# Expert 0 of a mixture of experts, started tile by tile inside the rounds of a linear attention

## The chip, the cores and the metric

One core of one Trainium2 chip. The time is device time of one launch in microseconds, the median of several runs; less is better. Profiles are of one further execution.

## The reference

A linear attention with decay feeds a mixture of experts. Sizes: 4 batches, 8 heads, 768 steps, head width 48; then 3072 tokens of width 384, 8 experts with hidden width 1024. All arrays are float32.

```python
for t in range(S):                       # attention, per batch and head
    cur = einsum('bhd,bhe->bhde', u * kt, vt)
    y[:, :, t] = einsum('bhd,bhde->bhe', rt, state + cur)
    state = w * state + einsum('bhd,bhe->bhde', kt, vt)
x = y.transpose(0, 2, 1, 3).reshape(3072, 384)
P = exp(x @ w_gate - max)                # gate
for _ in range(8):                       # Sinkhorn: rows, then columns
    P /= P.sum(1, keepdims=True) + 1e-9
    P /= P.sum(0, keepdims=True) + 1e-9
    P *= N / E
for e in range(E):                       # every expert on every token
    out += P[:, e:e+1] * (relu(x @ w1[e]) @ w2[e])
```

The gate needs all tokens, so it is known only after the whole attention. An expert's two products need only their tokens.

## The kernel before

**Tiles and rounds.** The 3072 tokens are 24 tiles of 128. Six tiles make a batch; the state S is carried from tile to tile within one. A loop of 27 rounds runs over the tiles with a lag, so that round i works on several tiles:

- `load_chunk(i+4)`: three DMAs on SyncE's queue for r, k, v of tile i+4. There are three buffers each for r and k and five for v, so the load of v waits until `stage_d(i-1)`, in the same round, is through with v of tile i-1.
- `prep(i+2)`: r and k times the decay tables `rtab` and `ktab` (r on GpSimd, k on VectorE: `rp`, `kp`).
- `bonus_dot(i+1)`, `bonus(i)`: the term with u, mostly GpSimd. It also adds `xadd`, the part of `hbx` that has been cleared to zero (the branch below may put something there).
- `stage_b(i+1)`: transposition of `rp` and `kp` on TensorE (`prT`, `pkT`), copied out by ScalarE.
- `scale_x(i-2)`, `stage_e(i-2)`: x of tile i-2 is split into a high and a low float16 part (`xsc`), and a DMA on SyncE's queue transposes it into `hbx`.
- `stage_c(i)`: products `pA` of transposed k and r, masked copies into `at` (VectorE), and the state's update (`pu`, S).
- `stage_d(i-1)`: `py`, the tile's output, on TensorE; then x, its largest magnitude and its scale on VectorE.
- `stage_f(i-3)`: the gate's logits `px`.

Every engine keeps the order in which the program issues its work, SyncE's queue too. The transposed blocks, `pA`, `pu` and `py` take turns in four PSUM banks.

**Expert 0 in the rounds.** TensorE is filled up with units of expert 0 (`work(n)`). Weights and activations are split into high and low float16 parts, so that each product takes three matmuls. `g1_unit(po, fc)` makes 128 of the 1024 hidden columns for position po, which is three tiles: 9 matmuls of 384 columns into `ph`, then ReLU on ScalarE (`hh`) and its low part on VectorE (`hl`). `g2_half(po, t, j)` multiplies half j of the hidden columns of one tile by w2: 12 matmuls into `po`, a copy and a DMA to `e0d`. Units of a position are listed when its three tiles are transposed. Units are worked on from round 5 on, two a round until round 8 and three from round 9 on; in earlier rounds `work` runs `spin(3)`, three matmuls on zeros that keep TensorE busy. What is left after the rounds runs in a loop that also does the Sinkhorn steps, and ten units and a rest inside the stages of the other experts.

**Steps beside the rounds.** `prepare()` takes the next step of a list; `STEPS` says how many steps a round takes before and after `stage_d`. First w1 of expert 0 is prepared, then w2 (largest magnitude in three pieces, reduction, exchange over partitions, scale, then high parts on ScalarE and low parts on VectorE), then combinations of tokens for the other experts (GpSimd additions). The latter begin in round 9.

**Start.** `hbx` is cleared by three engines. The tables come from a scan of w's powers on VectorE (`step`, `unit`, `pw`) and a reciprocal of all powers (`iv`), are transposed on TensorE (`pt_tab`) and copied out by ScalarE. If a decay lies outside [0.7, 1.1], a branch on `flag` (line 430) runs the attention of those channels step by step in `scan_channels`. With these inputs it isn't taken.

```python
for i in range(NTT + 3):
    ...
    work(1, i > 4)                 # after stage_e(i - 2)
    ...                            # bonus(i), stage_c(i)
    if i <= NTT:
        work(2 if i > 8 else 1, i > 4)
    ...                            # steps, stage_d(i - 1), steps, stage_f(i - 3)
    done = i - 2                   # the tile transposed in this round
```

Of the kernel before, what the change touches and what calls it, by code (L numbers as in the profile page):

```python
# [8 lines left out]
F32 = mybir.dt.float32  # L9
# [23 lines left out]
def rwkv_sinkhorn_moe(  # L33
# [117 lines left out]
    def split_weights(e, r1, r2, home):  # L151
# [11 lines left out]
        def rest_():  # L163
            pass

        for raw, wh, wl, j in ((r1, w1h, w1l, 0), (r2, w2h, w2l, 1)):
# [19 lines left out]
            def high(i, fl=fl, j=j, n=n):  # L186
                sl = slice(i * n, (i + 1) * n)
                S_.activation(fl[1][:, sl], fl[0][:, sl], AF.Copy, scale=sw[:, j : j + 1])

            def low(i, fl=fl, j=j, n=n):  # L190
                sl = slice(i * n, (i + 1) * n)
                V.scalar_tensor_tensor(
                    fl[2][:, sl], fl[0][:, sl], sw[:, j : j + 1], fl[1][:, sl],
                    op0=ALU.mult, op1=ALU.subtract,
                )

            steps = [lambda i=i, f=amax: f(i) for i in range(KC)] + [reduce_max, rest_, across, rest_, scale]
            for i in range(KC + 1):
                fs = [lambda i=i, f=high: f(i)] if i < KC else []
                fs += [lambda i=i, f=low: f(i - 1)] if i else []  # L200
                if i >= KC - 1:
                    fs.append(lambda i=i, j=j: split_done.add((("w1", "w2")[j], i - KC + 1)))
                steps.append(lambda fs=fs: [f() for f in fs])
            pieces += steps
# [9 lines left out]
    def g1_unit(po_, fc, W):  # L214
# [3 lines left out]
        hh, hl = h0(fc // FHC)  # L218
        ph = ps1.tile([P, TB], F32, tag="ph", name=f"ph_{po_}_{fc}")[:, :TB0]
# [3 lines left out]
        for c in range(KC):  # L223
# [6 lines left out]
            if c == KC - 1:  # L230
                fl = fc % FHC
                S_.activation(hh[:, fl, :], ph, AF.Relu)
                V.scalar_tensor_tensor(
                    hl[:, fl, :], ph, 0.0, hh[:, fl, :], op0=ALU.max, op1=ALU.subtract
                )
            yield

# [22 lines left out]
    def whole(gen):  # L260
        for _ in gen:
            pass
# [14 lines left out]
    wrow = part(hb3, F32, 2112, (H, D))[:1]  # L277
    wr = w.rearrange("(p two) d -> two d p", two=2)
    S_.dma_start(wrow, w.rearrange("(o h) d -> o h d", o=1))
# [14 lines left out]
    loads = {}  # L294

    def load_part(tt, nm, src):
        b, c = divmod(tt, NCHB)
        if tt == 3 and nm != "v":
            t_ = part(hb3, F32, 2880 + "rk".index(nm) * H * D, (H, D))
        else:  # L300
            t_ = ld.tile([P, H, D], F32, tag=nm + "n", name=f"{nm}n_{tt}", bufs=5 if nm == "v" else 3)
# [7 lines left out]
    raws = (part(ws0, F32, 0, (KC, F)), part(ws0, F32, KC * F, (FC, DM)))  # L309
    for tt in range(2):  # L310
        load_part(tt, "r", r)
        load_part(tt, "k", k)

    ub = ac.tile([P, H, D], F32, name="ub")
    wg = ac.tile([P, KC, E], F32, name="wg")

    load_part(0, "v", v)
# [3 lines left out]
    )  # L321
    load_part(2, "r", r)
    load_part(2, "k", k)
    load_part(1, "v", v)
    load_part(3, "r", r)
    load_part(3, "k", k)
    Q.dma_start(wg, w_gate.rearrange("(c p) e -> p c e", p=P))
    for c in range(KC):
        Q.dma_start(raws[0][:, c], w1[0, c * P : (c + 1) * P, :])


    N1 = HP + 1
    tmp = hb3
    step, unit, pw, iv = (
        tmp[:, i * NPAIR * N1 : (i + 1) * NPAIR * N1].rearrange("p (a n) -> p a n", n=N1)
        for i in range(4)
    )
    G.memset(hbx[:, :HB], 0.0)
# [3 lines left out]
    V.memset(hbx[:, HB : 2 * HB], 0.0)  # L342
# [8 lines left out]
    fill(hbx[:, 2 * HB :])  # L351
    spin(19)
# [8 lines left out]
    )  # L361
    maski = mask.bitcast(I32)
# [8 lines left out]
    for t_ in ss_:  # L371
        for j in range(2):
            G.memset(t_[j * HP : (j + 1) * HP, :, 1 - j, :], 0.0)
# [4 lines left out]

    wlim = part(hb3, F32, 2496, (H, D))[:1]
    flag = ac.tile([1, 1], F32, name="flag")  # L380
    V.tensor_scalar(wlim, wrow, W_MAX, W_MIN, op0=ALU.min, op1=ALU.max)
    V.tensor_tensor(wlim, wlim, wrow, op=ALU.not_equal)
    V.tensor_reduce(flag, wlim, axis=AX.XY, op=ALU.max)


    def scan_channels(scratch):
# [7 lines left out]
        Q.dma_start(wn, w.rearrange("(o h) d -> o (h d)", o=1).broadcast_to([D, H * D]))  # L394
# [12 lines left out]
        with tc.For_i(0, S, 1) as t:  # L407
            for dst, src in ((kb, k), (rb, r)):
                Q.dma_start(
# [3 lines left out]
            Q.dma_start(vt, v.rearrange("b h s d -> s d (b h)")[bass.ds(t, 1)].rearrange("o d a -> (o d) a"))  # L413
            V.tensor_tensor(rb, rb, stt, op=ALU.mult)
            V.tensor_reduce(yv, rb, axis=AX.X, op=ALU.add)
            for b in range(B):
                Q.dma_start(
# [8 lines left out]
        for t in range(NTT):  # L426
            Q.dma_start(xadd(t), yt[:, t, :])

    bad = nc.values_load(flag.bitcast(I32), min_val=0, max_val=0x3F800000)
    with tc.If(bad > 0):  # L430
# [3 lines left out]
    load_part(2, "v", v)  # L434
    load_part(3, "v", v)


    wsafe = ac.tile([P, NPAIR], F32, name="wsafe")
    good = ac.tile([P, NPAIR], F32, name="good")
    V.tensor_scalar(wsafe, wt, W_MAX, W_MIN, op0=ALU.min, op1=ALU.max)  # L440
    V.tensor_copy(step[:, :, 1:], wsafe.unsqueeze(2).broadcast_to([P, NPAIR, HP]))
    V.tensor_tensor_scan(
        pw.rearrange("p a n -> p (a n)"), step.rearrange("p a n -> p (a n)"),
        unit.rearrange("p a n -> p (a n)"), 0.0, op0=ALU.mult, op1=ALU.add,
    )

    V.tensor_tensor(good, wt, wsafe, op=ALU.is_equal)
    V.reciprocal(iv, pw)
    tab, tabr = (part(hb3, F32, 1040 + i * NPAIR * C, (NPAIR, C)) for i in range(2))
# [806 lines left out]
```

## Time and profile before

| what | value |
|---|---|
| median of 3 runs | 1536.81 us (1536.73 to 1538.33) |
| the profiled execution | 1537.3 us, its span 1535.4 us |
| TensorE (PE) busy | 1519.8 us, 99% of the span |
| VectorE (DVE) | 1033.7 us, 67% |
| ScalarE (ACT) | 663.5 us, 43% |
| GpSimd (POOL) | 598.1 us, 39% |
| DMA | 143.12 MB, mean 93 GB/s |

All operations of the kernel are recorded on one line, L29 (the helper that keeps program order), so groups are told apart by the names of their tiles. An arrow `a<-b` reads: a is written from b. A bracket at a row's end gives the engine's idle time before it and what ended it. Matmuls are pipelined; the pitch from one start to the next tells more than the length of one. SP is SyncE, and a q behind an engine's name is its instruction queue.

### The profile page before, as it was taken

What the parts mean: (1) busy time and instruction counts of PE and PEld (TensorE: products, weight loads), DVE (VectorE), ACT (ScalarE), POOL (GpSimd) and SP (SyncE); (2) the same over time, 40 slices, a digit from 0 to 9 for tenths busy, and PEclk for the clock granted to TensorE, in tenths of its full rate; (3) what the DMA queues carried; (4) which work ended last, traced back from release to release, by engine and by line L of the source; (5) the groups of instructions that cost most, each with busy time, mean ns of one, the idle gap of its engine ahead of it and who ended that gap; (6) DMA issues with size and microseconds to landing.
All of it is one profiled execution on the core that took longest, in us unless ns stands there. A gap on an engine that the chain in (4) does not pass through costs nothing.

```text
span 1535.4 us, 26169 instructions
## 1 busy us (share of the span) xinstructions
PE 1519.8 (99%) x10313; PEld 858.1 (56%) x10313; DVE 1033.7 (67%) x1714; ACT 663.5 (43%) x1168; POOL 598.1 (39%) x708
## 2 busy tenths in 40 slices
PE   8999999999999999999999999999999999999999
PEld 5677766655555555555555555555555555555555
DVE  8988877676666666667666666656666566666554
ACT  4333424434444444535454444535344444445320
POOL 8789985120213424242424324242423224242200
PEclk9999999999999999999999999999999999999999
DMA  8556623121225665675666666655445554555434
GB/s 192 104 114 113 131 49 112 51 73 55 98 58 109 88 118 86 110 107 83 116 92 125 92 117 88 126 64 98 58 62 92 61 98 56 98 60 98 55 95 129
DMA packets 186847, 143.12 MB, mean 93 GB/s; under 512 B 109537, under 2 KB 180962, under 8 KB 186722
## 3 DMA queue, kind: packets, MB, share of 16 engines
q0 software_dynamic: 44928, 61.36, 32.6%
q1 hardware_dynamic: 141584, 80.07, 19.8%
q8 instruction: 81, 1.33, 0.4%
q14 instruction: 44, 0.36, 0.1%
q10 hardware_dynamic: 210, 0.00, 0.0%
HBM read 55.39 MB, written 80.23 MB: 88 GB/s over the span
## 4 chain that ended last, share of the span: by engine, by line
PE 94%; DVE 5%; issue 0%; ACT 0%; DMA 0%; DVEq 0%; ACTq 0%
PE po L29 48%; PE bZ L29 12%; PE bY L29 12%; PE ph L29 5%; PE bA L29 5%; PE bB L29 5%; PE bC L29 2%; PE py L29 2%; PE pA L29 1%; DVE hb L29 1%; PE prT L29 1%; PE pu L29 1%; DVE at L29 0%; DVE ws L29 0%; PE pkT L29 0%
## 5 line engine op out<-in xcount | busy, mean ns | idle before, releaser
L29 PE MATMUL po<-ws,hbx 128*128 128x384 f16 x3360 | 736.8, 326 | 0.0
L29 POOL DMA_DIRECT2D accd<-stg x288 | 249.7, 869 | 694.4 <-ACT stg L29 673.8
L29 PEld LDWEIGHTS <-hbx 128*128 128x128 f16 x3504 | 334.1, 98 | 292.6
L29 PEld LDWEIGHTS <-ws 128*128 128x128 f16 x3096 | 301.8, 98 | 246.7 <-issue 3.4
L29 ACT ACTIVATE hbx<-tb 128x512 f16<-128x512 f32 x224 | 141.0, 630 | 451.6 <-DVE tb L29 451.6
L29 PE MATMUL po<-ws,hb 128*128 128x384 f16 x1248 | 323.0, 326 | 0.3 <-DVE ws L29 0.3
L29 DVE TENSOR_TENSOR tb<-bY,tb 128x512 f32<-128x512 f32 x168 | 116.1, 691 | 195.4 <-PE bY L29 195.2
L29 ACT ACTIVATE stg<-po,pe 128x384 f32<-128x384 f32 x312 | 179.1, 574 | 121.2 <-PE po L29 94.3
L29 PE MATMUL bZ<-xv,ws 128*128 128x512 f16 x840 | 227.0, 379 | 0.7 <-DVE tb L29 0.7
L29 PE MATMUL bY<-xv,ws 128*128 128x512 f16 x840 | 227.0, 379 | 0.0
L29 DVE TENSOR_TENSOR tb<-bZ,tb 128x512 f32<-128x512 f32 x168 | 115.4, 687 | 136.3 <-PE bZ L29 136.3
L29 PEld LDWEIGHTS <-hb 128*128 128x128 f16 x1248 | 121.4, 98 | 93.8 <-issue 0.8
L29 POOL TENSOR_TENSOR ucb<-rawb 128x256 f32<-128x256 f32 x84 | 75.7, 952 | 118.7 <-DMA rawb<-in_moe_w_dram 118.7
L29 DVE TENSOR_TENSOR tb<-bB,tb 128x512 f32<-128x512 f32 x112 | 77.4, 691 | 48.9 <-PE bB L29 47.0
L29 PE MATMUL ph<-hbx,ws 128*128 128x384 f16 x576 | 105.8, 329 | 1.2 <-DMA hbx<-xsc 0.7
L29 DVE SCALAR_TENSOR_TENSOR hb<-tb,hbx 128x512 f16<-128x512 f32 x112 | 77.2, 689 | 24.7 <-ACT hbx L29 19.5
L29 PE MATMUL bB<-xv,ws 128*128 128x512 f16 x336 | 90.8, 379 | 0.0
L29 PE MATMUL bA<-xv,ws 128*128 128x512 f16 x336 | 90.8, 379 | 0.0
L29 DVE SCALAR_TENSOR_TENSOR hbx<-tb,hbx 128x512 f16<-128x512 f32 x112 | 78.7, 703 | 14.7 <-ACT hbx L29 10.4
L29 ACT COPY tb<-bZ 128x512 f32<-128x512 f32 x56 | 32.8, 585 | 65.5 <-PE bZ L29 65.5
L29 ACT ACTIVATE hb<-ph 128x384 f16<-128x384 f32 x64 | 31.1, 488 | 57.6 <-PE ph L29 57.0
L29 DVE SCALAR_TENSOR_TENSOR hb<-ph,hb 128x384 f16<-128x384 f32 x64 | 35.4, 553 | 26.3 <-ACT hb L29 25.8
(166 smaller groups left out, 1539.6 us busy)
## 6 DMA issues: line engine op xcount, KB each, us to landing
accd<-stg POOLq DMA_DIRECT2D x288, 192.0 KB, 3.7
rawb<-in_moe_w_dram SPq DMA_DIRECT2D x28, 768.0 KB, 6.7
e0d<-stg SPq DMA_DIRECT2D x48, 192.0 KB, 2.1
hb<-e0d SPq DMA_DIRECT2D x48, 192.0 KB, 3.9
vn<-in_v_dram SPq DMA_DIRECT2D x24, 192.0 KB, 3.6
accd<-stg SPq DMA_DIRECT2D x24, 192.0 KB, 1.8
accd<-hb POOLq DMA_DIRECT2D x24, 192.0 KB, 4.7
rawb<-accd SPq DMA_DIRECT2D x24, 192.0 KB, 2.5
```

The lines of the kernel that those rows point to most:

```text
L29: return lambda *a, **k: self.tc.keep_in_program_order(f(*a, **k))
```

## The change

**Start.** The tables are built ahead of the branch in the program. One scan now runs over w and 1/w together, so the reciprocal is taken of w alone. The flag comes from the same columns through a small matmul on ones (`pnb`) instead of from a row of w of its own. VectorE clears five tiles of `hbx`, GpSimd eleven in pieces, ScalarE the last eight; VectorE also clears the state's off-diagonal blocks. The branch's DMAs are issued by GpSimd instead of SyncE.

**Loads.** All loads of tiles 0 to 4, r and k of tile 5, and both weights of expert 0 are issued ahead of the branch, w1's three pieces among tiles 0 and 1. r and k of tiles 3, 4 and 5 get places of their own (`hb3`, `xv0`). v of tile 5 is loaded in round 1, and from round 2 on round i loads tile i+4 as before.

**w1 and w2.** High and low parts are made in two pieces instead of three, each a half of the hidden columns. A first step stands behind `prep(0)`, a second behind `prep(1)`, and the new `STEPS` has w1 ready at the end of round 2, the first half of w2 at the end of round 5 and the second in round 6. In round 0 the order of `prep`, `bonus` and `stage_b` differs.

**Expert 0.** Position 0 is done tile by tile: `g1_tile(t, j)` makes half j of the hidden columns of tile t with 36 matmuls of 128 columns into one bank. Two of them are listed in the round in which tile t is transposed, and `work` uses them from round 3 on: tile t in round t+3, once ahead of `stage_c` and once after. The six `g2_half` of position 0 follow in rounds 6 to 8. Rounds 9 to 11 now have two units instead of three; from round 12 on there are three. ReLU and the low part of a unit are issued later, by `leave()`: ahead of the next unit, or behind the steps that precede `stage_d`.

```diff
@@ split_weights
+            def half(x_, i, j=j):
+                return x_[:, i * FHC : (i + 1) * FHC] if j else x_[:, :, i * FH : (i + 1) * FH]
...
+            pieces += [lambda i=i, f=amax: f(i) for i in range(KC)] + [reduce_max, across, scale]
+            pieces += [lambda f=high: f(0), lambda h=high, l=low: (h(1), l(0)), lambda f=low: f(1)]
@@ new
+    def g1_tile(t, j, W):
...
+        ph = ps1.tile([P, TB], F32, tag="ph", name=f"pht_{t}_{j}")
+        ph = ph.rearrange("p (f q) -> p f q", q=P)
+        for fl in range(FHC):
+            fs = slice((j * FHC + fl) * P, (j * FHC + fl + 1) * P)
+            for c in range(KC):
+                xh_, xl_ = xall(t, 0)[:, c, :], xall(t, 1)[:, c, :]
+                T.matmul(ph[:, fl], w1h[:, c, fs], xh_, start=(c == 0), stop=False)
+                T.matmul(ph[:, fl], w1h[:, c, fs], xl_, start=False, stop=False)
+                T.matmul(ph[:, fl], w1l[:, c, fs], xh_, start=False, stop=(c == KC - 1))
+        exits.append((hh, hl, ph))
+    def leave():
+        while exits:
+            hh, hl, ph = exits.pop(0)
+            S_.activation(hh, ph, AF.Relu)
+            V.scalar_tensor_tensor(hl, ph, 0.0, hh, op0=ALU.max, op1=ALU.subtract)
@@ whole(gen)
+        leave()
@@ loads
     for tt in range(2):
         load_part(tt, "r", r)
         load_part(tt, "k", k)
+    load_w1(0)
     ...                              # u
     load_part(0, "v", v)
+    load_w1(1)
+    load_w1(2)
+    load_part(1, "v", v)
     load_part(2, "r", r)
     load_part(2, "k", k)
     ...                              # w_gate
+    load_part(2, "v", v)
+    for tt in (3, 4):
+        load_chunk(tt)
+    Q.dma_start(raws[1], w2[0].rearrange("(c p) d -> p c d", p=P))
+    load_part(5, "r", r)
+    load_part(5, "k", k)
@@ start
-    G.memset(hbx[:, :HB], 0.0)
-    V.memset(hbx[:, HB : 2 * HB], 0.0)
+    V.memset(hbx[:, : Z[1]], 0.0)
+    clear_tiles(5, 11)
...
-    V.reciprocal(iv, pw)
+    V.reciprocal(wsi[:, 1], wsafe)
@@ scan_channels
-                Q.dma_start(
+                G.dma_start(
@@ rounds
     STEPS = {
-        0: (2, 2), 1: (0, 2), 2: (3, 1), 3: (1, 1),
-        4: (1, 1), 5: (1, 1), 6: (2, 2), 7: (1, 1), 8: (1, 1),
+        0: (3, 0), 1: (0, 2), 2: (1, 1), 3: (2, 1), 4: (1, 0), 5: (1, 3), 6: (1, 0), 7: (0, 0), 8: (0, 0),
     }
+    FIRST = TH
...
-        work(1, i > 4)
+        work(1, i >= FIRST)
...
-            work(2 if i > 8 else 1, i > 4)
+            work(2 if i > 11 else 1, i >= FIRST)
...
+        leave()
         if 1 <= i <= NTT:
             stage_d(i - 1)
...
+        if 0 <= done < TH:
+            units += [g1_tile(done, j, W) for j in range(2)]
+        if done == TH - 1:
+            units += [g2_half(0, t, j, W) for j in range(2) for t in range(TH)]
```

186 lines of the change are left out of this document (95 added, 91 removed).

## The prediction

> **What bounds the kernel now.** I read the page's busy times and slices first, then busy time by stretch, then TensorE's order of work, and last SyncE's queue. The page:
>
> ```profile
> PE 1519.8 (99%) x10313; PEld 858.1 (56%) x10313; DVE 1033.7 (67%) x1714; ACT 663.5 (43%) x1168; POOL 598.1 (39%) x708
> ```
>
> TensorE is the bound nearly everywhere; where it isn't must lie in the 1% left, which the next view finds at the front. I cut the front at each round's first transposition (prT): round 3 begins at 32.35, round 4 at 43.09, round 5 at 50.82, round 6 at 60.30, round 9 at 83.43, round 12 at 113.39. Columns of the next view: stretch, length, then busy us of each engine with its instructions, granted TensorE clock, DMA share, GB/s.
>
> ```profile
> 14.88:32.35 17.47, 16.96 (x281) 12.63 (x280) 16.92 (x32) 5.01 (x9) 16.92 (x18) 1.00 0.84 235
> 32.35:43.09 10.74, 8.12 (x117) 5.72 (x117) 9.96 (x24) 5.01 (x7) 8.86 (x10) 0.84 0.89 167
> 50.82:60.30 9.48, 8.73 (x113) 5.55 (x113) 9.25 (x19) 2.77 (x5) 7.14 (x10) 0.82 0.38 73
> 60.30:83.43 23.13, 22.52 (x377) 16.91 (x374) 22.10 (x51) 10.58 (x18) 15.59 (x17) 1.00 0.54 105
> 83.43:113.39 29.96, 29.62 (x419) 21.11 (x417) 25.86 (x50) 9.88 (x19) 25.26 (x26) 1.00 0.55 107
> 113.39:300.00 186.61, 186.11 (x2129) 126.19 (x2126) 150.46 (x302) 74.77 (x136) 134.50 (x147) 1.00 0.43 94
> 300.00:1500.00 1200.00, 1199.32 (x6559) 641.98 (x6558) 767.42 (x1188) 542.87 (x958) 374.15 (x455) 1.00 0.54 88
> ```
>
> From 83.43 on TensorE idles 0.34 + 0.50 + 0.68 us in 1417. So the change is worth this and little else: when round 9 begins, and how much expert-0 work ("units") is done by then. Before that VectorE sets the pace (22.10 of 23.13 us in rounds 6 to 8), TensorE having only two units a round. One full round and two halves of w2 products give the prices (start, length; the pitch is the distance to the next start):
>
> ```profile
> 75.87 0.64 PE L29 MATMUL prT<-ident,rp 128*128 128x128 f32 x4
> 76.34 0.60 PE L29 MATMUL pkT<-ident,kp 128*128 128x128 f32 x4
> 76.78 1.63 PE L29 MATMUL ph<-hbx,ws 128*128 128x384 f16 x9
> 78.33 1.10 PE L29 MATMUL pA<-rT,kT 64*64 64x128 f32 x32
> 79.37 0.67 PE L29 MATMUL pu<-vn,kp 128*64 128x48 f32 x16
> 79.97 1.64 PE L29 MATMUL ph<-hbx,ws 128*128 128x384 f16 x9
> 81.54 0.88 PE L29 MATMUL py<-S,rT 128*64 128x96 f32 x16
> 82.25 1.09 PE L29 MATMUL py<-vn,at 128*64 128x48 f32 x32
> 83.27 0.30 PE L29 MATMUL px<-wgp,hbx 128*128 128x16 f16 x6
> 88.59 4.06 PE L29 MATMUL po<-ws,hb 128*128 128x384 f16 x24
> ```
>
> Round 8 is 7.56: two w1 units of 1.55 and 1.57, and 4.44 of attention. Two w2 half units take 4.06 with the tail of the pipeline, 2.0 each. Without pu (a batch's last tile) attention is 3.84, without py from S (its first) 3.73.
>
> **The change, part by part.** The unit counts first. Before, 8 w1 units of position 0 run in rounds 5 to 8. After, six tile units run in rounds 3 to 5 and all six w2 halves of position 0 in rounds 6 to 8; rounds 9 to 11 then have two units instead of three. From round 9 on 104 units remain before and 98 after: six w2 halves fewer, 6 x 2.0 = **-12.0 us**. That is the whole gain on offer; all else is when round 9 begins.
>
> *Start and tables.* These rows carry the table chain and its consumers:
>
> ```profile
> 2.27 2.62 DVE L29 MEMSET hbx<- 128x3072 f32 x1 [0.59 <-issue]
> 6.98 0.17 DVE L29 TENSOR_SCALAR wsafe<-wt 128x4 f32<-128x4 f32 x1 [0.74 <-DVE flag L29]
> 7.53 0.70 DVE L29 TENSOR_TENSOR_SCAN hb<-hb 128x260 f32<-128x260 f32 x1
> 8.96 1.76 DVE L29 RECIPROCAL hb<-hb 128x260 f32<-128x260 f32 x1
> 14.03 3.16 DVE L29 TENSOR_TENSOR kp<-kn,ktab 128x384 f32<-128x384 f32 x3 [1.98 <-ACT ktab L29]
> 31.47 1.36 DVE L29 COPY_PREDICATED at<-mask,pA 128x512 f32<-128x512 int32 x2
> ```
>
> The clearing shrinks to 1920 of 3072 columns (-0.98), the 260-column reciprocal to 4 columns (-1.6), the scan doubles (+0.7): kp of tile 0 at 12.1. If the 2.09 us between the clearing's end (4.89) and wsafe leave the chain too, 10.0. I take 11. From there to the end of tile 2's masked copies was 18.8 us; the same work stands there after (the three maxima of w1 included), plus a wait for r2 and k2, which now queue behind all of w1. I take 19.5: round 3 at 30.5 (29 to 32; before 32.35). POOL's clearings (16 tiles less five on VectorE and eight on ScalarE) stay ahead of its first use of a table.
>
> *The loads.* SyncE's queue, and the DMA rate in 40 slices of 1.5 us:
>
> ```profile
> 12.79 1.77 SPq L29 DMA_DIRECT2D ws<-in_moe_w_dram  x3
> 21.02 1.28 SPq L29 DMA_DIRECT2D vn<-in_v_dram  x2
> 37.62 1.49 SPq L29 DMA_TRANSPOSE hbx<-xsc  x1
> ...
> L430 SPq EVENT_SEMAPHORE  x8: 17/17/17, 18.7 to 20.6; - x8
> L430 DVEq COMPARE_BRANCH  x1: 67/67/67, 14.0 to 14.0; - x1
> ...
> GB/s 0 16 218 213 183 176 147 198 198 158 339 404 270 3 39 152 236 189 172 373 383 292 132 170 218 129 170 169 89 119 154 20 223 131 150 5 0 67 197 9
> ```
>
> At the branch SyncE sits from 14.56 to 21.02 and the DMAs stand still for some 2.5 us (the slices 3 and 39). With the branch's DMAs moved to POOL and all loads ahead of it I count that as gone. But tile 0's transposition, the first input of expert 0, still has seven tiles' r, k, v and both weights ahead of it on that queue: 37.62, less 2.5, plus 3.1 to landing = **38.2** (36 to 41). In the kernel before, nothing waited for it then.
>
> *Round 3.* TensorE has its transpositions done at 31.4 and then stands at the first tile unit until 38.2, with pA of tile 3 queued behind it. Then 36 matmuls of 128 columns. No row has that form. Below lies px, 0.16/6 = 0.027 each for 16 columns; above, 0.172 for 384. A third of the latter is 0.057; I take 0.060, 2.2 a unit (1.0 to 6.2). So round 4 begins at 38.2 + 2.2 + 1.04 + 0.60 + 2.2 + 1.73 + 0.16 = 46.1: **+3.0** (-0.2 to +6). On the warm price alone the Trainium skill speaks ("TensorE: Matmul & The Clock Gate", "Wait — 56ns, not 53.3ns?"): about 55.6 ns from start to start for 128 columns, by which a unit would be an estimated 2.0 us; no run here shows it yet.
>
> *Rounds 4 and 5.* The lag is what costs. The load of v(i+4) waits on SyncE's queue for py(i-1) of the same round (five buffers), and tile i-2 is transposed behind it:
>
> ```profile
> 48.86 0.31 PE L29 MATMUL px<-wgp,hbx 128*128 128x16 f16 x6
> 50.82 0.63 PE L29 MATMUL prT<-ident,rp 128*128 128x128 f32 x4 [1.65 <-DVE at L29]
> 52.76 0.50 PE L29 MATMUL ph<-hbx,ws 128*128 128x384 f16 x1 [0.75 <-DMA hbx<-xsc]
> 48.97 0.37 SPq L29 DMA_DIRECT2D vn<-in_v_dram  x1
> 49.60 1.22 SPq L29 DMA_TRANSPOSE hbx<-xsc  x1
> ```
>
> py is over when px starts at 48.86, v goes at 48.97, the transposition at 49.60 lands at 52.76: 3.6 to 3.9 us. TensorE reaches the first unit of the next round 0.16 + 0.91 = 1.1 after py. Before, that hit once; after, each of rounds 4 and 5 opens with the tile just transposed and waits 2.5. Round 4: 4.44 + 4.4 + 2.5 = 11.3; round 5: 3.84 + 4.4 + 2.5 = 10.7.
>
> *Round 6.* Its first w2 half needs the low part of w2, now one piece of 1536 columns issued at the end of round 5, after x of tile 4:
>
> ```profile
> 68.36 0.53 DVE L29 TENSOR_TENSOR x<-py,rk 128x384 f32<-128x384 f32 x1
> 70.34 0.17 DVE L29 RECIPROCAL sw<-isw 128x1 f32<-128x1 f32 x1
> 75.13 2.18 ACT L29 ACTIVATE ws<-ws,sw 128x1024 f16<-128x1024 f32 x2
> 84.57 1.27 DVE L29 SCALAR_TENSOR_TENSOR ws<-ws,sw,ws 128x1024 f16<-128x1024 f32 x1
> 87.39 2.02 DVE L29 SCALAR_TENSOR_TENSOR ws<-ws,sw,ws 128x1024 f16<-128x1024 f32 x1
> ```
>
> From x to the scale 2.15, the high part 1.5 x 1.09 = 1.6, the low part 1.5 x (1.27 to 2.02) = 1.9 to 3.0: 6.2 after py, where TensorE is ready at 1.1. It waits 5.1 (4 to 6). Round 6: 4.44 + 4.0 + 5.1 = 13.5. Rounds 7 and 8, w2 halves that touch no VectorE: 3.73 + 4.0 and 4.44 + 4.0. Rounds 4 to 8 sum to 51.6; before they took 83.43 - 43.09 = 40.3: **+11.3**.
>
> *The clock.* In 50.82:60.30 the granted clock is 0.82, a loss of 0.18 x 9.48 = 1.7 us, and the row at 50.82 and 52.76 shows what came before: idle 1.65 and 0.75. Four such waits (rounds 3 to 6) cost 0 to 4 x 1.7; part of a slow stretch is spent waiting, so I take **+3.0**. The Trainium skill ("TensorE: Matmul & The Clock Gate", "Part 1: The HAM clock gate") halves the clock after an idle window of about 3.4 us. By it only rounds 3 and 6 would be slowed, the term would be half as large and the sum an estimated +5.0. The trace does not agree so far, since 2.4 us of idle time in two pieces were enough.
>
> *Rounds 9 to 11.* Two units leave TensorE 4.44 + 3.1 = 7.6 a round, while rounds 9 to 11 hold 25.86/3 = 8.6 us of VectorE and 25.26/3 = 8.4 of POOL work (tokens being prepared). Up to 1.0 a round is lost, nothing if these engines lag without being waited for: **+1.2** (0 to 3).
>
> *With one answer.* The moved evacuations (leave) put ReLU and its low part after the masked copies: nothing, as two banks take turns and two units lie between; if that cover fails, 0.25 a group of units, the length of one wait for a late operand. Three units fewer in the loop after the rounds: TensorE stays full there. The order of w1's preparation: on VectorE the same columns as before.
>
> Sum: +3.0 + 11.3 + 3.0 + 1.2 - 12.0 = **+6.5 us** on the profiled execution's 1537.3 (span 1535.4), which is 0.5 above the median shown. That gives 1536.8 + 6.5, **1543**. A measurement of this kernel tells about 0.2%, 3.1 us, from no change.
>
> **The rivals.** *Faster: the waits are hidden.* If tiles arrive and w2's low half is done before TensorE asks, the 2.5 + 2.5 + 5.1 and the 3.0 of clock go, and round 4 begins with before's: 1.2 - 12.0 + 11.3 - 10.1 = -9.6, **1527**. VectorE being the pace before speaks for it (its work by round 9 hardly grows); the order on SyncE's queue against it. It decides where the waits and clock losses of rounds 3 to 6 fall below half of what I count. *No change: half of them*, **1537**. *Slower still*: the standstill at the branch remains (+2.5), every wait brings its slow stretch (+3.8), rounds 9 to 11 lose 3: **1551**. *The tables' move does nothing*: VectorE's branch stands at 14.0 already, behind the tables' last step, so moving the source above the branch may free no compute engine. Round 3 would begin near 32; tile 0 decides it anyhow, so the time stays **1543**. *Only the long waits slow the clock*, those of round 3 (7 us) and round 6 (5 us): two rounds of four, 1.5 instead of 3.0, **1542**; the row with 0.82 behind 2.4 us of idle time speaks against it. That is how the Trainium skill's rule on the clock, above, would have it.
>
> **How the numbers follow.** My case 0.35, with the tables' move doing nothing 0.10, with only long waits slowing the clock 0.08, slower still 0.10, no change 0.17, faster 0.20. The likeliest's own range is 1537 to 1549 (tile 0 at 36 or 41, clock 0 to 6.8). For 8 in 10 I go from 1530 to 1551. Slower 0.63, same 0.17, faster 0.20.
>
> **What would show it.** Right: tile units opening rounds 4 and 5 with a wait of 2 to 3 us for the DMA of hbx, round 6's first w2 half with one of 4 to 6 for VectorE's ws, a granted clock below 0.9 in rounds 3 to 6, round 9's first transposition near 101 and TensorE full behind it. Wrong: round 9 before 92, or no such waits; then the gain stands. A pitch of the 36 matmuls above 0.08 would add over 4 us; TensorE idle between rounds 12 and 26 would mean that the saved work buys nothing.

## The result and the profile after

The changed kernel takes **1551.88 us** (1550.62 to 1552.92) against 1536.77 us (1536.52 to 1538.33) before, measured side by side: ratio 1.0096, 95% interval 1.0078 to 1.0113. It is 15.1 us slower. I had forecast 1543, slower by 6.5, with a range to 1551: the sign was right, the size was less than half.

The kernel before stood at 1536.7 to 1536.9 in every comparison below, so the times can be set side by side. The busy times on the page after:

```profile
PE 1522.5 (98%) x10441; PEld 866.5 (56%) x10441; DVE 1026.8 (66%) x1715; ACT 663.0 (43%) x1164; POOL 596.2 (38%) x712
```

The page hides the loss: TensorE is 98% busy instead of 99%. The same cut at the rounds' first transpositions shows it. Busy times by stretch, columns as before: rounds 0 to 2, then 3, 4, 5, 6, then 7 and 8, 9 to 11, and 12 up to the first product of the other experts:

```profile
11.31:36.72 25.41, 19.85 (x280) 14.61 (x281) 18.31 (x41) 7.81 (x13) 19.22 (x20) 0.88 0.86 207
36.72:49.80 13.08, 10.76 (x185) 9.96 (x183) 12.12 (x18) 4.50 (x7) 10.51 (x9) 0.84 0.31 63
49.80:63.51 13.71, 10.39 (x189) 9.60 (x185) 8.78 (x20) 2.89 (x5) 6.02 (x7) 0.88 0.37 59
63.51:76.37 12.86, 10.37 (x176) 9.42 (x172) 7.20 (x16) 2.89 (x5) 4.77 (x5) 0.87 0.31 64
76.37:90.90 14.53, 10.54 (x141) 6.79 (x137) 8.99 (x18) 5.47 (x7) 4.78 (x5) 0.88 0.27 55
90.90:107.31 16.41, 16.41 (x258) 11.97 (x255) 11.78 (x27) 5.30 (x10) 11.95 (x14) 1.00 0.75 147
107.31:131.73 24.42, 22.89 (x378) 16.99 (x375) 23.59 (x48) 8.48 (x16) 17.79 (x20) 1.00 0.52 109
131.73:324.56 192.83, 190.35 (x2146) 128.42 (x2146) 149.32 (x305) 75.59 (x138) 137.24 (x150) 1.00 0.36 92
```

Round 3 begins at 36.72 (before 32.35), round 4 at 49.80 (43.09), round 9 at 107.31 (83.43). There the kernel is 23.9 us behind. The other experts' first product (bA), in the trace after and then in that of before:

```profile
324.56 0.81 PE L29 MATMUL bA<-xv,ws 128*128 128x512 f16 x3
```

```profile
308.54 0.81 PE L29 MATMUL bA<-xv,ws 128*128 128x512 f16 x3
```

That is 16.0 behind: 7.9 came back, out of the 12.0 of saved work. In rounds 3 to 6 each stretch loses twice, by waiting (in round 4 TensorE is busy 10.39 of 13.71) and by the clock (0.84 to 0.88).

The waits, in TensorE's order of work, with the releaser in brackets:

```profile
40.48 3.67 PE L29 MATMUL pht<-hbx,ws 128*128 128x128 f16 x36 [2.33 <-DMA hbx<-xsc]
45.79 2.18 PE L29 MATMUL pht<-hbx,ws 128*128 128x128 f16 x36
47.91 0.88 PE L29 MATMUL py<-S,rT 128*64 128x96 f32 x16
54.19 3.72 PE L29 MATMUL pht<-hbx,ws 128*128 128x128 f16 x36 [3.31 <-DMA hbx<-xsc]
67.06 3.01 PE L29 MATMUL pht<-hbx,ws 128*128 128x128 f16 x36 [2.49 <-DMA hbx<-xsc]
79.90 0.32 PE L29 MATMUL po<-ws,hb 128*128 128x384 f16 x1 [2.46 <-ACT ws L29]
81.75 3.63 PE L29 MATMUL po<-ws,hb 128*128 128x384 f16 x11 [1.53 <-DVE ws L29]
131.73 0.66 PE L29 MATMUL prT<-ident,rp 128*128 128x128 f32 x4 [1.43 <-POOL rp L29]
278.37 1.64 PE L29 MATMUL ph<-hbx,ws 128*128 128x384 f16 x9 [0.49 <-DVE hb L29]
283.73 0.34 PE L29 MATMUL po<-ws,hb 128*128 128x384 f16 x1 [1.93 <-DVE hb L29]
```

A unit of 36 matmuls at full clock goes from 45.79 to 47.91, 2.12 us, 0.059 a matmul. The same unit takes 3.67 and 3.72 behind the waits of rounds 3 and 4. The transposition whose landing ends these waits, on SyncE's queue, for tile 0 and then tile 1, and below it the last step of its input on VectorE:

```profile
30.21 1.34 SPq L29 DMA_DIRECT2D kn<-in_k_dram  x1
36.86 0.37 SPq L29 DMA_DIRECT2D vn<-in_v_dram  x1
37.43 1.34 SPq L29 DMA_TRANSPOSE hbx<-xsc  x1
...
49.81 0.37 SPq L29 DMA_DIRECT2D vn<-in_v_dram  x1
50.30 1.22 SPq L29 DMA_TRANSPOSE hbx<-xsc  x1
...
33.10 0.62 DVE L29 SCALAR_TENSOR_TENSOR xsc<-x,xs,xsc 128x384 f16<-128x384 f32 x1 [2.44 <-ACT xsc L29]
43.77 0.61 DVE L29 SCALAR_TENSOR_TENSOR xsc<-x,xs,xsc 128x384 f16<-128x384 f32 x1
```

The queue stands from 31.55 to 36.86 at the load of v of tile 6, which needs the buffer that py of tile 1 is reading; the transposition of tile 0 goes right behind it. Tile 0 was ready at 33.72 and tile 1 at 44.38, so they lay 3.7 and 5.9 us before their transpositions were issued at 37.43 and 50.30.

The clock, last. It was granted at half speed in six stretches of 3.41 us near the front. Busy times in the stretch ahead of two of them, and in those two themselves (the clock is the third column from the end):

```profile
37.47:40.88 3.41, 1.08 (x14) 0.88 (x13) 3.27 (x7) 2.01 (x4) 3.41 (x2) 1.00 0.72 147
51.12:54.53 3.41, 0.34 (x7) 0.38 (x8) 3.27 (x9) 1.04 (x2) 2.00 (x2) 1.00 1.23 187
...
40.88:44.29 3.41, 3.41 (x36) 3.21 (x37) 3.41 (x3) 0.64 (x2) 2.47 (x2) 0.50 0.45 91
54.53:57.94 3.41, 3.41 (x37) 3.21 (x38) 0.74 (x2) 0.00 (x0) 1.83 (x2) 0.50 0.21 39
```

TensorE was busy 1.08 and 0.34 us of the stretch ahead, and then worked 3.41 us at 0.50. An estimate of the price is half of the 3.41, up to 1.7 us on top of each of these waits.

### The profile page after: what moved, and what is told of

Read it like the earlier page. It is cut to its first block, busy times and chain, and to the rows that moved or that the text cites. A ratio compares the mean times of both kernels' runs of the same rounds, so it can differ in the third digit from the quotient of the medians.

```text
span 1551.1 us, 26486 instructions
## 1 busy us (share of the span) xinstructions
PE 1522.5 (98%) x10441; PEld 866.5 (56%) x10441; DVE 1026.8 (66%) x1715; ACT 663.0 (43%) x1164; POOL 596.2 (38%) x712
## 3 DMA queue, kind: packets, MB, share of 16 engines
q8 instruction: 82, 1.34, 0.4%
## 4 chain that ended last, share of the span: by engine, by line
PE 93%; DVE 4%; POOL 1%; issue 1%; DMA 1%; ACT 0%; SPq 0%; DVEq 0%; POOLq 0%; ACTq 0%
PE po L29 48%; PE bZ L29 12%; PE bY L29 12%; PE bA L29 5%; PE bB L29 5%; PE ph L29 4%; PE bC L29 2%; PE py L29 2%; PE pA L29 1%; PE pht L29 1%; DMA hbx<-xsc 1%; PE pz L29 1%; PE pu L29 1%; PE prT L29 0%; POOL rk L29 0%
## 5 line engine op out<-in xcount | busy, mean ns | idle before, releaser
L29 PEld LDWEIGHTS <-ws 128*128 128x128 f16 x3240 | 310.5, 99 | 249.7 <-issue 10.1
L29 DVE SCALAR_TENSOR_TENSOR hb<-tb,hbx 128x512 f16<-128x512 f32 x112 | 77.2, 690 | 24.6 <-ACT hbx L29 19.5
L29 PE MATMUL ph<-hbx,ws 128*128 128x384 f16 x504 | 91.5, 326 | 0.6 <-DVE hb L29 0.5
L29 ACT COPY stg<-po 128x384 f32<-128x384 f32 x48 | 22.9, 477 | 69.9 <-PE po L29 62.4
L29 DVE SCALAR_TENSOR_TENSOR ws<-ucb,sw,ws 128x768 f16<-128x768 f32 (+1 forms) x56 | 51.8, 945 | 1.2 <-ACT ws L29 1.2
```

What stands on the lines that cost most here:

```text
L29: return lambda *a, **k: self.tc.keep_in_program_order(f(*a, **k))
```

## The experiments

**The loads behind the transposition.** My first theory was that the order on SyncE's queue makes the waits of rounds 3 to 5. Alone changed: from round 2 on the loads of tile i+4 are issued behind the transposition of tile i-2.

```diff
-            elif 1 < i < NTT - 4:
-                load_chunk(i + 4)
             ...
             stage_e(i - 2)
             emitted[0] = i - 1
+        if 1 < i < NTT - 4:
+            load_chunk(i + 4)
```

> The changed kernel with one edit: from round 2 on the loads of tile i+4 are issued behind the transposition of tile i-2 instead of ahead of it. Theory (the waits of rounds 3 to 5 come from SyncE's queue, where the transposition stands behind a load of v that waits for py): the first units of rounds 4 and 5 wait no longer (3.3 and 2.5 us), that of round 3 waits at most for w1's low half at 39.1 (1 instead of 2.3 us), and the slow clock behind the three waits goes, some 1.6 us each: 7 + 4.8, about 11 us less, 1541. Rival (VectorE sets the pace of these rounds, the waits hide behind it): TensorE waits for masked copies instead, 4 us less or nothing, 1548 to 1552.

Measured: 1543.02 us (1542.81 to 1544.03), ratio to before 1.0043 (1.0026 to 1.0059). That is 8.9 less than the changed kernel. TensorE's waits for its first units in rounds 3 and 4, and rounds 3 to 5 by stretch:

```profile
39.39 2.07 PE L29 MATMUL pht<-hbx,ws 128*128 128x128 f16 x34 [2.37 <-DVE ws L29]
48.97 2.17 PE L29 MATMUL pht<-hbx,ws 128*128 128x128 f16 x36 [0.87 <-DMA hbx<-xsc]
```

```profile
35.70:47.03 11.33, 8.96 (x185) 8.14 (x183) 10.62 (x21) 4.43 (x7) 9.53 (x9) 1.00 0.53 75
47.03:56.72 9.69, 8.82 (x189) 8.13 (x186) 9.52 (x18) 2.77 (x5) 5.80 (x7) 1.00 0.46 92
56.72:66.68 9.96, 8.63 (x176) 7.98 (x172) 8.61 (x20) 2.77 (x5) 7.25 (x9) 1.00 0.61 122
```

Rounds 4 and 5 take 9.69 and 9.96 us instead of 13.71 and 12.86, at a full clock. Round 5 waits no longer for its tile; a wait of 1.33 us for VectorE is left there, in front of a small matmul (pmax_w, at 64.28). In round 3 the wait is as long as before but for something else, w1's low part on VectorE, where I had expected 1 us; that is some 1.4 of the 2 us by which 8.9 falls short of the 11 expected. No slow stretch follows this wait of 2.37 us (the last section says why). The waits of round 6 stay. So more than half of the loss of 15.1 is the place of a tile's loads in a queue, with the slow clock that the waits brought.

**Only the clock.** Matmuls on zeros are put in front of the first unit of rounds 3 to 6, where TensorE waits; nothing is removed.

```diff
+        if i in SPIN:                 # {3: 10, 4: 12, 5: 10, 6: 10}
+            spin(SPIN[i])
         work(1, i >= FIRST)
```

> The changed kernel with one edit: matmuls on zeros fill the waits, 10, 12, 10 and 10 of 512 columns ahead of the first unit of rounds 3, 4, 5 and 6 (2.2 to 2.6 us each, no longer than the wait). Theory (every one of these waits is followed by a slow stretch of 3.4 us that costs about 1.6 us): the granted clock stays at 1.00 from round 4 to round 6, the waits end when they did, 5 to 6.5 us less, 1546. Rival (as predicted, half of the slow stretches hides behind other waits): 3 us less, 1549. Second rival (the matmuls on zeros run past the end of the wait): no change or slower.

Measured: 1546.01 (1545.95 to 1547.41), ratio 1.006 (1.0043 to 1.0077): 5.9 less than the changed kernel. Rounds 3 to 6 of its trace:

```profile
36.11:47.82 11.71, 11.00 (x196) 9.09 (x193) 11.00 (x21) 4.54 (x7) 9.91 (x9) 1.00 0.36 71
47.82:59.87 12.05, 11.41 (x201) 9.27 (x197) 10.82 (x22) 2.89 (x5) 7.76 (x10) 1.00 0.36 67
59.87:71.14 11.27, 10.93 (x185) 8.88 (x182) 7.21 (x16) 2.89 (x5) 4.77 (x5) 1.00 0.36 73
71.14:85.62 14.48, 12.64 (x150) 7.79 (x147) 9.01 (x18) 5.47 (x7) 4.80 (x5) 0.88 0.27 56
```

In rounds 3 to 5 the clock is whole; in round 6 the zeros were too few for a wait of 4 us, and a slow stretch remained. Rounds 3 to 5 are 1.4, 1.7 and 1.6 shorter although they hold ten or twelve matmuls more: 4.6 us for three slow stretches and nothing else. (Another 0.6 of the 5.9 is that round 3 begins earlier in this trace; the rest isn't assigned.)

**w2 one round earlier.** Its steps are issued one round earlier, still ahead of the evacuations: `4: (2, 0), 5: (3, 1), 6: (0, 0)`.

> The changed kernel with one edit in the table of steps: w2's maximum goes over the partitions in round 4, its scale, high parts and first low half are issued ahead of stage_d in round 5 and the second low half behind it. Theory (round 6 opens with a wait of 4.0 us for w2's first high and low half, and with the slow clock behind it): both waits go, 4.0 + 1.6, about 5.5 us less, 1546.5. Rival (VectorE's 1.8 us ahead of x of tile 4 only move the wait to the next masked copies or x): 1 us less or nothing, 1551 to 1552.

Measured: 1551.44 (1550.47 to 1551.68), ratio 1.0093 (1.0077 to 1.011). The time is the rival's, but the way is not the one it named. The chain stands at the head of two engines' queues and holds what lies behind it:

```profile
74.30 3.81 PE L29 MATMUL pht<-hbx,ws 128*128 128x128 f16 x36 [1.99 <-DVE hb L29]
...
78.46 0.16 DVE L29 TENSOR_SCALAR isw<-pmax_w 128x1 f32<-128x1 f32 x1 [4.21 <-PE pmax_w L29]
...
79.04 3.04 ACT L29 ACTIVATE ws<-ws,sw 128x1536 f16<-128x1536 f32 x2 [7.12 <-DVE sw L29]
```

VectorE stands 4.21 us at the scale's first step, which needs a matmul that TensorE does only after round 5's second unit. Behind it, on VectorE and on ScalarE, lies the evacuation of a unit of tile 2. And the exchange takes its place in one of the two PSUM banks of the units (`ph`), here from its first matmul in round 4 (61.81) until this step has read it at 78.46. So both units of round 5 share the other bank, and the second waits 1.99 us until VectorE has evacuated the first, with a unit at half clock behind it (3.81). Round 6 got shorter (9.73 us) and round 5 longer (16.35).

**w2's chain in the gaps of round 5.** The same steps once more, each where its engine is idle: the maximum over the partitions behind the first unit, the scale behind `stage_c`, high and low parts ahead of `stage_d`.

```diff
+    PRE, MID = {5: 1}, {5: 1}
         work(1, i >= FIRST)
+        steps(PRE.get(i, 0))
         ...                           # bonus, stage_c
+        steps(MID.get(i, 0))
-        5: (1, 3), 6: (1, 0)
+        5: (2, 0), 6: (1, 0)
```

> The changed kernel with w2's scale and halves alone moved: the maximum over the partitions behind round 5's first unit, the scale behind its masked copies, high and low parts ahead of stage d of round 5 (in the changed kernel: behind it). Theory (round 6's waits of 2.46 and 1.53 us go, and the slow stretch behind them; ScalarE and VectorE are idle in round 5 while TensorE waits for the tile): 1546.2 to 1548. Rival (as with one round earlier, the preparation holds an evacuation and round 5 loses what round 6 gains): 1550.5 to 1552.

Measured: 1546.62 (1545.41 to 1547.62), ratio 1.0062 (1.0047 to 1.0077), 5.3 less. In its trace round 6 holds no wait over 0.5 us. The bank still costs something: round 5's second unit waits 1.16 us for the scale's step (isw) that reads it. What failed in the first attempt was the place within the round, not the idea.

**The front.** Three edits of the first three rounds. First `prep(2)` alone, moved to the head of round 0 as it was before the change.

> The changed kernel with one edit: prep(2) stands at the head of round 0 again, ahead of the bonus of tile 0, as in the kernel before. Theory (round 3 began 6 us later than forecast, partly because GpSimd now makes rp of tile 2 only after it has waited for dg of tile 0): the transposition of tile 2 starts by 19.5 instead of 21.1 and round 4 begins 1.5 to 3 us earlier, 1549 to 1550.5. Rival (r2 and k2 arrive late behind w1, so GpSimd and VectorE wait for them in place of dg): no gain, as VectorE then stands before the masked copies of tile 0, 1552 or above.

Measured: 1552.0 (1551.4 to 1554.42), ratio 1.0104 (1.0087 to 1.0121): no gain, as the rival had it. GpSimd then waits for the load, with all that is behind it in its queue:

```profile
16.14 0.99 POOL L29 TENSOR_TENSOR rp<-rn,rtab 128x384 f32<-128x384 f32 x1 [3.32 <-DMA rn<-in_r_dram]
```

Second, w1's first high part alone, half a round later: `1: (0, 1), 2: (2, 1)` for `1: (0, 2), 2: (1, 1)`.

> The first high part of w1 is issued in the middle of round 2 instead of at the end of round 1; nothing else moves. Theory (ScalarE was held by it for 6.3 us in front of tile 2's copies, which put 1.41 us on pu and 2.44 us on xsc in round 2): those two waits go, round 3 begins near 34.5 instead of 36.7, and the time is 1549.5 to 1550. Rival (w1's low part then comes later and tile 0's first unit waits for it instead of for its DMA): round 3 begins earlier, its first unit no earlier than 40.5, time 1551.5 to 1552.

Measured: 1550.45 (1549.34 to 1553.74), ratio 1.0087 (1.007 to 1.0103). That lies between the two expectations and doesn't decide. In the profiled execution the wait in front of pu is gone, but round 1 began 3.4 us later than in the changed kernel, so that its round 3 (37.78) can't be compared.

Third, all of the front together:

```diff
     load_part(0, "v", v)
+    load_part(2, "r", r)
+    load_part(2, "k", k)
     load_w1(1)
-    load_w1(2)
     load_part(1, "v", v)
-    load_part(2, "r", r)
-    load_part(2, "k", k)
+    load_w1(2)
...                     # prep(2) at the head of round 0; two maxima of w1 behind
...                     # stage_c(0); its exchange over partitions behind stage_c(1);
...                     # its first high and low parts ahead of gate_split in round 2
```

> The changed kernel with only its first three rounds rearranged: r and k of tile 2 ahead of w1's second and third block and prepared at the head of round 0, two of w1's maxima behind tile 0's masked copies, the maximum over the partitions behind tile 1's pA, w1's first parts in the middle of round 2. Theory (round 3's first unit comes 3.6 us after py of round 2 whatever is on the queue, so each us by which round 3 begins earlier is a us of the time): round 3 near 32.5 instead of 36.7, time 1547 to 1549. Rival (the DMA queue's backlog holds tile 0's transposition, as the prediction had it): the wait in round 3 grows by what the round begins earlier, 1551 to 1552.

Measured: 1546.88 (1546.78 to 1547.47), ratio 1.0066 (1.005 to 1.0081), 5.0 less. Round 3 begins at 32.38 instead of 36.72, and its first unit comes at 36.06 after the same wait as ever:

```profile
36.06 2.17 PE L29 MATMUL pht<-hbx,ws 128*128 128x128 f16 x36 [2.59 <-DMA hbx<-xsc]
```

The tile came 4.4 us earlier, as py of tile 1 did. No backlog of loads held it. What each of the edits adds isn't shown: alone, the two that were tried gained nothing and an undecided 1.4.

**The new start with the old units.** The other half of the change by itself: the start, the loads and w1 in the gaps as changed, but position units of 384 columns from round 5 on and w2 spread over rounds 3 to 8, as before.

> The changed kernel's start (loads, tables, clearing, branch, w1 in the gaps) with the old expert-0 work: position units of 384 columns from round 5 on, evacuated at once, and w2 prepared over rounds 3 to 8. Theory (the new start costs by itself, round 3 beginning 4.4 us later, and the one wait of 2.4 us in round 5 takes up part of it): 1539 to 1541.5. Rival 1 (rounds 3 to 5 have slack enough to take it up): 1536.5 to 1537.5. Rival 2 (all of the loss is of the tile units): 1535 or less, since the table chain is shorter.

Measured: 1539.99 (1539.09 to 1541.71), ratio 1.0022 (1.0012 to 1.0032). So the start costs 3.3 us by itself, and the tile units, with the late evacuation, the two units a round and the earlier preparation of w2 that came with them, 11.9 on top of it.

**The late evacuation.** `g1_unit` evacuates when its last matmul is issued, as before.

> The units of positions 1 to 4 are evacuated when their last matmul is issued, as in the kernel before; only the tile units of position 0 still leave through the list. Theory (the late evacuation cost 0.49 and 1.93 us behind the rounds, at 278.37 and 283.73): those waits shrink to the 0.50 that the kernel before had, 1549.7 to 1550.2. Rival (the wait there is for something else, or more work in the rounds takes it back): 1551.5 to 1552.

Measured: 1552.11 (1551.45 to 1556.9), ratio 1.011 (1.0093 to 1.0127). The waits at 278 and 283 are gone from its trace and the time isn't shorter: round 12 opens with a wait of 1.67 us for GpSimd there, and behind it stands a slow stretch of the clock that the changed kernel didn't have. The theory was neither shown nor refuted. With three units a round from round 9 on (`work(2 if i > 8 else 1, ...)`), so that TensorE doesn't stand there:

> The immediate evacuation of the units of positions 1 to 4 once more, now with three units a round from round 9 on, so that TensorE does not stand in round 11. Theory (the late evacuation does cost 1.9 us, which the slow stretch behind the 1.67 us of wait in round 11 hid in the first trial): neither wait nor slow stretch in rounds 9 to 11, 1548 to 1549. Rival (the immediate evacuation buys nothing): 1550.4 to 1550.8, only round 11's 1.4 less.

Measured: 1546.83 (1546.44 to 1548.89), ratio 1.0067 (1.0052 to 1.0083), below both expectations. Its trace has five slow stretches near the front where the changed kernel's has six: two in round 3 and none in round 4, in spite of a wait of 3.20 us there. So part of the gain is the clock's. Waits and clock must be kept apart for such small terms.

**All repairs together.** Loads behind the transposition, tile 2 first, w1 and w2 later and earlier, immediate evacuation of position units:

> All repairs together: r and k of tile 2 loaded ahead of the second and third block of w1 and prepared at the head of round 0, all but one maximum of w1 behind tile 0's masked copies, w1's first high part in the middle of round 2, the loads of tile i+4 behind the transposition of tile i-2, w2's preparation one round earlier with its products ahead of the evacuations, position units evacuated at once. Theory: 1543.0 for the load's place alone, less 2 to 3 for round 3 beginning near 34, less 4 to 5 for round 6, less 2 for the evacuation: 1533 to 1536, faster than the kernel before. Rival (each wait taken away uncovers the next one, VectorE's in round 3 first): 1538 to 1542.

Measured: 1536.43 (1534.95 to 1540.55), ratio 0.9999 (0.999 to 1.0009): as fast as before, between the two expectations. Its longest waits up to round 8:

```profile
20.70 0.28 PE L29 MATMUL pmax_w<-ident,wma 128*1 128x128 f32 x1 [2.95 <-DVE wma L29]
36.73 0.28 PE L29 MATMUL pht<-hbx,ws 128*128 128x128 f16 x2 [1.61 <-ACT ws L29]
38.58 3.35 PE L29 MATMUL pht<-hbx,ws 128*128 128x128 f16 x34 [1.57 <-DVE ws L29]
56.80 0.27 PE L29 MATMUL pmax_w<-ident,wma 128*1 128x128 f32 x1 [2.46 <-DVE wma L29]
```

All four end with VectorE or ScalarE at steps of the weights' preparation, two of them in front of the small matmul of the exchange over partitions (pmax_w), which TensorE meets in its order before VectorE has the input. Those four are treated in the next kernel, with three units from round 9 on; its steps stand in the gaps, `PRE, MID = {5: 1}, {1: 1, 2: 2, 5: 1}`.

> The kernel with all repairs (1536.4), with its own remaining waits addressed: w1's maximum over the partitions moved from the end of round 0 behind tile 1's pA (2.95 us of wait in front of tile 2's transpositions), w1's first high and low parts ahead of the gate's split in round 2 (1.61 and 1.57 us in round 3), w2's maximum over the partitions from round 4 into round 5 (2.46 us), and three units a round from round 9 on (1.65 us of POOL's lag). Theory (each wait that goes shortens the front, and two slow stretches of the clock go with them; VectorE is busy 69.8 of the 82.8 us there, so up to 13 can go): 1529 to 1532, faster than the kernel before. Rival (VectorE's queue puts each wait somewhere else, as it did when w2 came one round earlier): 1535 to 1537.

Measured: **1530.52** (1530.02 to 1531.6), ratio to before 0.9959 (0.9946 to 0.9973), 6.3 us faster than the kernel before the change. Rounds 3, 4, 5, and 6 to 8:

```profile
30.61:42.02 11.41, 9.19 (x187) 8.15 (x183) 10.70 (x21) 2.97 (x6) 9.56 (x8) 1.00 0.61 85
42.02:52.23 10.21, 8.81 (x188) 8.12 (x185) 9.98 (x20) 2.77 (x5) 6.33 (x9) 1.00 0.45 87
52.23:63.36 11.13, 8.60 (x175) 8.02 (x172) 9.71 (x22) 5.70 (x7) 7.06 (x8) 1.00 0.54 108
63.36:88.32 24.96, 24.96 (x392) 18.30 (x389) 20.91 (x42) 7.90 (x15) 16.80 (x19) 1.00 0.57 129
```

The clock is whole in all of the front. Round 9 begins at 88.32, still 4.9 later than before the change, with six w2 halves done. One thing limits what the 6.3 says of the tile units: the kernel before has slow stretches of its own, in rounds 3 and 5 (granted clock 0.84 and 0.82 in the profile before), by the same estimate worth up to 3.4 us. No run shows the kernel before with a whole clock there, so how much of the 6.3 is the clock's stays open.

**One part put back at a time.** Into this kernel, whose clock is whole, first the late evacuation:

> The fastest kernel so far (1530.5, no slow stretch of the clock in its trace before the end) with one thing put back: the units of positions 1 to 4 leave late again. Theory (the late evacuation costs what its wait behind the rounds showed, 1.93 and 0.49 us, less the 0.33 that is there with the immediate one): 1532 to 1532.8. Rival (other work takes the wait up): 1530.2 to 1530.9.

Measured 1532.98 (1531.94 to 1534.34), 2.5 more: it does cost. The waits for VectorE's hb in its trace are 0.84, 0.29 and 1.34 us. Of its nine executions, the four with a mean clock of 1.000 took 1531.9 to 1532.3, 1.4 to 1.8 more than 1530.5, and the others 1533.0 to 1534.3, so about a microsecond of the 2.5 comes by the clock. Then two units a round in rounds 9 to 11:

> The fastest kernel so far with two units a round again in rounds 9 to 11 instead of three. Theory (POOL's lag shows as a wait of 1.4 to 1.7 us at the start of round 12): 1531.9 to 1532.3, and 1.7 more if a slow stretch follows it. Rival (the third unit only moves work, and POOL's lag is gone since the front is shorter): 1530.2 to 1530.9.

Measured 1532.82 (1531.55 to 1535.23), 2.3 more; round 12 opens at 112.81 with a wait of 1.65 us for GpSimd's rp. Its executions fall in two groups, six at 1531.6 to 1532.8 and five, at a mean clock of 0.997 to 0.998, at 1534.6 to 1535.2, which fits the wait without and with slow stretches. Then the old order on SyncE's queue:

> The fastest kernel so far with the loads of tile i+4 ahead of the transposition of tile i-2 again. Theory (rounds 3 to 5 each wait 2.3 to 3.3 us again for the tile, where they wait 0.75, 1.40 and 0 now, and two or three of these bring a slow stretch of 1.7): 1537.5 to 1541. Rival (the waits alone, TensorE's clock stays): 1534.5 to 1536.5.

Measured 1538.66 (1537.67 to 1541.37), 8.1 more, with waits of 2.75, 3.42 and 2.47 us:

```profile
36.21 2.17 PE L29 MATMUL pht<-hbx,ws 128*128 128x128 f16 x36 [2.75 <-DMA hbx<-xsc]
48.44 3.80 PE L29 MATMUL pht<-hbx,ws 128*128 128x128 f16 x36 [3.42 <-DMA hbx<-xsc]
```

That one line of order turns 6.3 us faster into 1.8 slower (ratio 1.0014, 1.0005 to 1.0023).

The parts nearly add up. Repaired alone in the changed kernel they are worth 8.9 (queue), 5.3 (w2's place) and 5.0 (front); put back alone in the last kernel, 2.5 (evacuation) and 2.3 (units in rounds 9 to 11). That is 24.0, where all together gave 1551.9 - 1530.5 = 21.4. What the parts share isn't shown.

## Why the prediction was right in sign and short in size

The forecast of the sum was +6.5, and the other experts begin 16.0 later: 9.5 are missing. The mechanism, waits for the tile and for w2 with a slow clock behind them, was right. The steps that failed are three terms of the sum. Tile 0's transposition was put at 38.2 by a backlog of loads and landed at 40.48 behind py of tile 1, because the front was late (2.3 us). The slow clock was put at 3.0 and cost 6.3 (3.3 us). The late evacuation was put at nothing and cost some 1.9. These are 7.5 of the 9.5; another 1.0 is that the saved work was 11.0 and not 12.0. By the prediction's own steps:

- **Start and tables.** `kp` of tile 0 began at 10.70, forecast 11 (14.03 before): right, and against the rival by which the tables' move does nothing. The term behind it failed. I gave 19.5 us from there to the end of tile 2's masked copies; it took 24.7 (10.70 to 35.43). I had named the wait for r and k of tile 2 and sized it at less than 1 us; in the `prep(2)` experiment GpSimd stood 3.32 us for that load. What I hadn't looked for were w1's steps at the head of a queue. TensorE waited 2.31 us for w1's maximum in front of tile 2's transpositions, which then ran at half clock, and in round 2 ScalarE stood 6.29 us at w1's first high part with tile 3's copies behind it.

```profile
19.68 0.27 PE L29 MATMUL pmax_w<-ident,wma 128*1 128x128 f32 x1 [2.31 <-DVE wma L29]
...
30.01 1.58 ACT L29 ACTIVATE ws<-ws,sw 128x1536 f16<-128x1536 f32 x1 [6.29 <-DVE sw L29]
```

- **Round 3.** Right that the first unit waits for tile 0's transposition, wrong in why. I put the landing at 38.2 by the backlog of loads on the queue. SyncE's queue stood from 31.55 on with its loads done (no DMA moved from 34.05 to 37.46), and the landing at 40.48 was the end of py of tile 1 (36.79) plus 3.7, the rule that I had written down for rounds 4 and 5. So I took a late front as covered by the DMAs, and it was not: 2.3 us here, and 5.0 for the front's repair, clock included.
- **The tile unit.** Forecast 2.2 us, measured 2.12 at full clock. The Trainium skill's 55.6 ns between starts ("TensorE: Matmul & The Clock Gate", "Wait — 56ns, not 53.3ns?") gives an estimated 2.0 for 36. The trace's 0.059 us a matmul lies between it and my price of 0.060.
- **Rounds 4 to 6, the waits.** Forecast 2.5, 2.5 and 5.1, by the DMA of hbx twice and by ws once; measured 3.31, 2.49 and 2.46 + 1.53 = 4.0, by the same releasers. Right, 0.3 us off in sum. Putting the order back in the last kernel confirmed the cause of the first two, the w2 experiment that of the third.
- **The clock.** Forecast +3.0 of 0 to 6.8. The units' rows show 3.67 and 3.72 for 2.18, 3.01 with the pA behind it at 1.85 for 1.10, and eleven matmuls of a w2 half 3.63 where 1.95 would do (12 matmuls take 2.12): 1.5 + 1.5 + 1.6 + 1.7 = 6.3. Zeros in three of these waits gave 4.6 back. So the term was half of what it should have been. Of the rivals, "slower still" had it right that each of the four waits brings its slow stretch here; in other traces waits of 2.37 to 3.20 us brought none.
- **The rule on the clock.** In my reading of the Trainium skill ("TensorE: Matmul & The Clock Gate", "Part 1: The HAM clock gate") only rounds 3 and 6 would be slowed, as only those were to hold an idle time of a window's length. All four were, and in none was TensorE idle for a whole stretch: it worked 1.08, 0.34, 1.12 and 0.40 us of the 3.41 ahead. That reading is refuted; the length of the window agrees (3413 ns there, 3.41 in the trace).
- **Rounds 9 to 11.** Forecast +1.2, measured 1.53 idle (22.89 of 24.42), and 2.3 where it was put back alone.
- **The late evacuation.** Costed at nothing, with 0.25 a group if the cover fails. That cover was the wrong one: I looked at the rounds, where two units lie between, and not at the time behind the rounds, where a w2 half needs the low part that was just issued. It shows as 1.93 + 0.49 us in the trace, where the kernel before waits 0.50 in the same place (1.9 more), and as 2.5 where it was put back alone.
- **Six w2 halves fewer, -12.0.** Nearly right: from round 9 to the other experts TensorE was busy for 213.24 us instead of 224.27, 11.0 less, and idle for 4.01 instead of 0.84. So this part took 217.3 us instead of 225.1, 7.9 less.
- **The branch.** SyncE no longer stands there, as forecast, and I gave it the 2.5 us. It could give nothing here, since the queue's next stop was py of tile 1.

The range ended at 1551, the sum of "slower still". That sum had room for the clock (+3.8, and 3.3 came) but none for a late front or the late evacuation. Its other two parts, the branch (+2.5) and rounds 9 to 11 (+1.8), came to nothing and 0.3. That it ends only 0.9 below the measured time is luck.

## What to carry to other kernels

When a consumer is moved closer to its producer, follow the whole queue between them: here the tile was ready, but its transfer stood behind a load that waited for a buffer, and moving three loads a few lines down was worth 8 to 9 us. A preparation chain that crosses engines (maximum, exchange, scale, product) can hold everything issued behind its head on each of these queues, 4.21 us on VectorE and 7.12 on ScalarE here, and the bank in which it waits; place each link where its engine is idle and its input is there, not as a block. And price a wait on TensorE with the slow clock behind it, which was half as much again here (some 1.6 us on 2.3 to 4.0).

## What the hardware showed

The granted clock changes on a grid of 3.41 us. In the changed kernel slow stretches begin at 20.40, 34.05, 40.88, 54.53, 68.18 and 81.83, all a whole number of 3.41 us apart. The grid isn't tied to the kernel's start: with the loads behind the transposition the first slow stretch begins at 21.32, 0.92 later, though the two programs are the same up to round 2.

What went ahead of a slow stretch was little work on TensorE in one stretch of the grid, not a stretch without any. The first 150 us of the seventeen traces give a bound (two have no slow stretch, so that their grid can't be read). All 46 stretches at full clock in which TensorE was busy for at most 1.42 us were followed by a slow one, and none in which it was busy for more than 2.05. Between these both occur: 1.46 us, in the second trial of the immediate evacuation, was not followed by one, and 2.00 us in round 2 of the changed kernel was, at a wait of 1.41 and small matmuls:

```profile
30.64:34.05 3.41, 2.00 (x31) 1.33 (x29) 0.97 (x3) 2.42 (x4) 0.87 (x1) 1.00 0.79 156
...
34.05:37.46 3.41, 3.41 (x52) 3.32 (x48) 2.90 (x10) 0.79 (x2) 2.97 (x5) 0.50 0.00 0
```

The ends of matmuls in a trace are modelled, so these bounds are rough, and what decides between them these runs don't settle. In the fastest kernel single waits of 0.6 to 1.7 us left the clock at 1.00 throughout.

So the same wait may or may not be followed by a slow stretch: it matters how much of it falls into one stretch of the grid. The 2.33 us of round 3 left 1.08 us of work in one. The 2.59 us in the front's third experiment were cut in two by the grid at 35.00, which left 1.88 and 2.36, and the unit behind them ran at full clock (2.17 us). Ahead of round 12, 1.43 us left 2.00 in the changed kernel, and no slow stretch came; 1.67 with immediate evacuation left 1.74, and one did. As the grid isn't tied to the kernel, two edits of equal worth can differ by a slow stretch or two, up to 1.7 us each.
